# Attention logits in one visit to full-height matmuls per chunk, and two value loads moved in their queue

## The chip, the cores and the metric

The kernel runs on one NeuronCore of a Trainium2 chip. The metric is the device time of one execution in microseconds (us). TensorE is called PE in the profile (PEld are its weight loads), VectorE is DVE, ScalarE is ACT, GpSimd is POOL and SyncE is SP. POOL and SP issue nearly all DMAs here: what POOL issues runs on the queue that the profile calls q0, what SP issues on q1.

## What is computed

One block of a conditioned transformer: modulation rows from a condition `c`, a local dilated attention with 32 heads of 18 channels, and a bilinear gated feed-forward layer. S is 2048, D is 576, F is 4608, everything in bf16.

```python
mod = (silu(c) @ w_mod).reshape(1, 6, 1, -1)      # sa, ca, ga, sb, cb, gb
h = layernorm(x) * (1 + ca) + sa
q, k, v = split_heads(h @ wqkv)                    # H=32, Dh=18
idx = pos[:, None] - arange(8)[None, :] * 2        # 8 keys, 2 apart
logits = einsum('bhsd,bhswd->bhsw', q, k[idx]) * scale
attn = softmax(where(idx >= 0, logits, -1e9))
o = einsum('bhsw,bhswd->bhsd', attn, v[idx])
x = x + ga * (o @ wo)
h = layernorm(x) * (1 + cb) + sb
x = x + gb * (((h @ w_gate) * (h @ w_up)) @ w_down)
```

## The kernel before

**Tiling.** The rows are cut into 8 chunks of 256 (numbered 0 to 7) for the attention, and into five groups of 128-row tiles for the feed-forward layer (`GROUPS`: 256, 512, 512, 384 and 384 rows; group 0 to 4). For each group `gate_up` makes gate and up products for 36 column tiles f of F, then `down` multiplies by `w_down`. The attention of chunks 1 to 7 is cut into small pieces that are put between the column tiles of those two loops: chunks 1 and 2 in group 0, 3 and 4 in group 1, 5 and 6 in group 2, 7 in group 3. Everything is emitted by hand in one order, and each engine executes its own instructions in that order.

**The main loop, and its two kinds of matmuls.** `gate_up` computes with half-height matmuls (`half`, L523): the contraction is split into rows 0 to 63 and rows 64 to 127 of the array, two matmuls run at the same time, one for the gate and one for the up product. A column tile takes 9 such pairs. In the page these are `pg` and `pu`, line L524, form 64\*128. The attention pieces use all 128 rows: the logits (`b_lq`, L443) and the transposes (`b_lt`, L459).

**Attention of one chunk.** `b_p(i, w)` (L429) makes on DVE the product of q and of k shifted by window step w, one tile of 128 x 1280 in bf16 (L433); there are eight, and the pool `prodp` holds six. `b_lq(i, wq)` (L437) sums four of those products over the channels of a head with 20 matmuls against the 0/1 matrix `ind` into the PSUM tile `lg`, one half (wq = 0 or 1) of it at a time. After the second half ACT copies `lg` to `lgs` (L449). `b_lt` transposes `lgs` with four matmuls, then comes the softmax on DVE and ACT (`b_sm0`, `b_exp`, `b_sm1`), then the weighting of the shifted values by `b_mul` (L496) and their sum by `b_add`. The shifted values are loaded by `b_ld(i, j)` (L421, issued at L427 on POOL's queue: 1152 KB, one load for each half j of a chunk) into the two buffers `vsh` of `vshp`.

**Order.** `B_two` and `B_one` (L706, L710) write out the order of the pieces of two chunks, or of one, with a cost beside each (0.83 for a product, 0 for `b_lq`, and so on). `spread` (L735) places a piece at the column tile where the middle of its cost falls, in proportion to the sum of all costs. In column tile k PE runs the first half of tile k, the second half of tile k-1, and then the pieces of slot k; DVE runs the pieces of slot k and then the product `hh` of tile k-1 (L778), which waits for the two casts of ACT (L772, L773).

**Loads.** `load_wgu` (L145) loads a block of four column tiles of `w_gate` and `w_up` on SP's queue; three buffers, and `ahead` (L790) issues block n+2 when block n-1 is done. `load_wd` (L160) loads a block of `w_down` on POOL's queue, again three buffers. `behind(dma, load)` (L181) makes one DMA wait until a given load has landed. `gb_row` (L1144) runs in `down` of group 0, after its first tile: it makes the row `gb` from `wm5`, a tile that holds one of the three `w_down` buffers, and then issues the loads of `w_down` blocks 1 and 2 and the value loads of chunk 2.

Of the kernel before, what the change touches and what calls it, by code (L numbers as in the profile page):

```python
# [7 lines left out]
BF = mybir.dt.bfloat16  # L8
# [10 lines left out]
P = 128  # L19
D = 576  # L20
DP = 640
KT = 5
# [10 lines left out]
CH = 256  # L33
ST = CH // P
# [12 lines left out]
def kernel(  # L47
# [20 lines left out]
    def pool(name, bufs, **kw):  # L68
        return ctx.enter_context(tc.tile_pool(name=name, bufs=bufs, **kw))
# [6 lines left out]
    lnp = pool("lnp", 2)  # L76
# [4 lines left out]
    prodp = pool("prodp", 6)  # L81
# [10 lines left out]
    def ps(shape, dt, name):  # L92
        return psp.tile(shape, dt, name=name, tag="bank")
# [21 lines left out]
    oT = consts.tile([P, KT, CH], BF, name="oT")  # L115
# [13 lines left out]
    def x_rows(i):  # L129
        return x_flat[i * CH:(i + 1) * CH, :].rearrange("(j p) d -> p j d", p=P)  # L130

    def load_x(i):
        if i < NCH:
            x_in[i] = sp.tile([P, ST, D], BF, name="x_t1") if i == 1 else xin.tile([P, ST, D], BF, name="x_t")
            nc.sync.dma_start(x_in[i][:], x_rows(i))
# [5 lines left out]
    wgu_blk, wgu_in, wd_blk = {}, {}, {}  # L141
    NG = len(GROUPS)
    NBLK = FT // FB
# [16 lines left out]
    def load_wd(g):  # L160
        if g >= NG * NBLK - 4:
            return
        r0 = (g % NBLK) * FB * P
        wb = wdp.tile([P, FB, D], BF, name="wd")
        wd_blk[g] = wb
        return nc.gpsimd.dma_start(wb[:], B_w_down[r0:r0 + FB * P, :].rearrange("(k p) n -> p k n", p=P))  # L166
# [14 lines left out]
    def behind(dma, load):  # L181
        tc.add_manual_dep(dma.ins, load.ins.name, SYNC, reason="value rows go first")
# [93 lines left out]
    def layernorm(src, tag):  # L276
        xn, stat, rsq, norm = ln_parts(src, tag)
        for j in range(ST):
            stat(j)

        def norms(js=range(ST)):
            for j in js:
                norm(j)
        return xn, lambda: rsq(slice(0, ST)), norms
# [13 lines left out]
    def transposed(src, dst, cols, vi, between=None, kf=KF):  # L298
        n = P * len(cols)
        pA = ps([P, 3, n], BF, "tr_pA")  # L300
        pB = ps([P, 2, n], BF, "tr_pB")
        for c, j in enumerate(cols):
            if c and between:
                between()
            for m in range(KT):
                d = pA[:, m, :] if m < 3 else pB[:, m - 3, :]
                nc.tensor.transpose(d[:, js(c)], src[:, j, m * P:(m + 1) * P], ident[:])  # L307

        def evict(on_dve=(0, 1, 2)):
            for m in range(KT):  # L310
                s = pA[:, m, :] if m < 3 else pB[:, m - 3, :]
                modulate(dst(m), s, kf if m == KF else m, vi + 1, vi, m in on_dve)
        return evict
# [32 lines left out]
    def a_ln(i):  # L346
        x = x_in.pop(i)
        xn, rsq, norm = layernorm(lambda j: x[:, j, :], "a")
        aa[i] = dict(xn=xn, rsq=rsq, norm=norm)

    def a_norm(i):
        aa[i]["rsq"]()
        aa[i]["norm"]()

    def a_tiles(i):
        hT = hTp.tile([P, KT, CH], BF, name="hT") if i > 1 else vshp.tile([P, KT, CH], BF, name="vsh")
        aa[i].update(hT=hT, qT=qTs[i % 2], kT=kTs[i % 2])
# [8 lines left out]
    def a_t(i, on_dve=(0, 1, 2), between=None):  # L366
        a_tiles(i)
        hT = aa[i]["hT"]
        transposed(aa[i]["xn"], lambda m: hT[:, m, :], (0, 1), 0, between, KT if i in PAIRED else KF)(on_dve)
# [51 lines left out]
    def b_ld(i, j):  # L421
        b = bb.setdefault(i, dict(prod={}, vsh={}))
        base = HALO + i * CH + j * P - DIL * (W - 1)
        vsh = vshp.tile([P, W, DH, H], BF, name="vsh")
        vsrc = bass.AP(vd.tensor, vd.offset + base * D, [[D, P], [DIL * D, W], [1, D]])
        b["vsh"][j] = vsh
        return nc.gpsimd.dma_start(vsh[:].rearrange("p w d h -> p w (d h)"), vsrc)  # L427

    def b_p(i, w):  # L429
        b = bb.setdefault(i, dict(prod={}, vsh={}))  # L430
        off = HALO - DIL * (W - 1 - w)
        prod = prodp.tile([P, KT, CH], BF, name="prod")
        nc.vector.tensor_tensor(prod[:], aa[i]["qT"][:], aa[i]["kT"][:, :, off:off + CH], ALU.mult)  # L433
        b["prod"][w] = prod


    def b_lq(i, wq):  # L437
        b = bb[i]
        if wq == 0:
            b["lg"] = ps([P, 2, CH], F32, "lg")  # L440
        for m in range(KT):
            for wl in range(4):
                nc.tensor.matmul(b["lg"][H * wl:H * (wl + 1), wq, :], lhsT=ind[:, m, :], rhs=b["prod"][4 * wq + wl][:, m, :],  # L443
                                 start=(m == 0), stop=(m == KT - 1), skip_group_check=True)
        for wl in range(4):
            b["prod"].pop(4 * wq + wl)
        if wq == 1:
            lgs = lgp.tile([P, 2, CH], BF, name="lgs")
            nc.scalar.copy(lgs[:], b.pop("lg")[:])  # L449
            b["lgt"] = lgp.tile([P, 2, ST, 4, H], BF, name="lgt")  # L450
            b["lgs"] = lgs

    def b_lt(i):
        b = bb[i]
        lgs = b.pop("lgs")
        pt = ps([P, 2, ST, P], BF, "lt")
        for a in range(2):
            for j in range(ST):
                nc.tensor.transpose(pt[:, a, j, :], lgs[:, a, js(j)], ident[:])  # L459
        nc.scalar.copy(b["lgt"][:].rearrange("p a j w h -> p (a j w h)"), pt[:].rearrange("p a j n -> p (a j n)"))  # L460

    def b_sm0(i):
        b = bb[i]
        lg = b.pop("lgt")
        mx = smp.tile([P, ST, 4, H], BF, name="mx", tag="tree")
        dd = smp.tile([P, 2, ST, 4, H], F32, name="dd")
        nc.vector.tensor_tensor(mx[:], lg[:, 0], lg[:, 1], ALU.max)
        nc.vector.tensor_tensor(mx[:, :, 0:2], mx[:, :, 0:2], mx[:, :, 2:4], ALU.max)
        nc.vector.tensor_tensor(mx[:, :, 0], mx[:, :, 0], mx[:, :, 1], ALU.max)
        for wq in range(2):  # L470
            nc.vector.tensor_tensor(dd[:, wq], lg[:, wq], mx[:, :, 0:1].to_broadcast([P, ST, 4, H]), ALU.subtract)
        b["dd"] = dd
# [221 lines left out]
    def B_pr(i, w0, w1):  # L694
        return [(0.83, lambda w=w: b_p(i, w)) for w in range(w0, w1)]

    def B_lq(i, wq):
        return [(0.0, lambda: b_lq(i, wq))]

    def B_sm(i, beside=None):  # L700
        return [(0.5, lambda: (b_lt(i), beside and beside())),  (1.2, lambda: b_sm0(i)), (0.8, lambda: b_exp(i)), (0.4, nop), (1.8, lambda: b_sm1(i))]

    def B_wait(us):
        return [(us, nop)]

    def B_two(a, b, av_a, av_b, turned=None):  # L706
        return (B_pr(a, 0, 6) + B_lq(a, 0) + B_pr(a, 6, 8) + B_pr(b, 0, 2) + B_lq(a, 1) + B_pr(b, 2, 6) + B_sm(a, lambda: b_lq(b, 0))
                + B_pr(b, 6, 8) + av_a[:4] + B_lq(b, 1) + av_a[4:] + B_sm(b, (lambda: a_t(turned)) if turned else None) + av_b)

    def B_one(a, ld, av_a):  # L710
        return B_pr(a, 0, 4) + ld[:1] + B_pr(a, 4, 6) + B_lq(a, 0) + B_pr(a, 6, 8) + ld[1:] + B_wait(1.5) + B_lq(a, 1) + B_wait(4.0) + B_sm(a) + av_a

    def B_av(i):
        r = []
        for j in range(ST):
            r += [(0.7, lambda j=j, w=w: b_mul(i, j, w)) for w in range(0, W, 2)]
            r += [(0.7, lambda j=j: b_add(i, j, 0)), (0.7, lambda j=j: b_add(i, j, 1)), (1.2, lambda j=j: b_add(i, j, 2))]
            if i in (3, 5):
                r.append((0.0, lambda j=j: b_ld(i + 1, j)))
        return r  # L720
# [402 lines left out]
    def res(i):  # L1123
        return (0.0, lambda: load_res(i))

    def values(i):
        return [(0.0, lambda: [b_ld(i, j) for j in range(ST)])]

    gbg = {0: B_two(1, 2, B_av(1) + [res(2), (0.0, load_wm5), (0.0, lambda: load_wd(0))], []),
           1: values(3) + B_two(3, 4, B_av(3) + [res(3), res(4), (2.4, lambda: a_ln(5)), (1.2, lambda: (a_norm(5), load_x(7)))], B_av(4), 5),  # L1130
           2: values(5) + B_two(5, 6, B_av(5) + [res(5), res(6)], B_av(6)),
           3: B_one(7, [(0.0, lambda j=j: b_ld(7, j)) for j in range(ST)], B_av(7)) + [res(7)],
           4: [(1.0, nop), (1.0, early_wd)]}
    av2 = [p for _, p in B_av(2)]
    oq = out_qkv(1, 3)
# [8 lines left out]
    def gb_row():  # L1144
        mod_row(lambda p, k: wm5[p, k, :] if k < KF else wm5r[p, :], gb_bc, sc_bc2)()
        behind(load_wd(1), wgu_in[4])
        behind(b_ld(2, 0), wgu_in[7])
        b_ld(2, 1)
        load_wd(2)

    dbg = {0: [gb_row] + first + out_qkv(2, 4) + [load_pair_rows],
           1: out_qkv(3, 5) + out_qkv(4, 6),
# [43 lines left out]
```

## Time and profile before

| | us |
|---|---|
| median of 3 runs | 558.31 (557.96 to 561.82) |
| the profiled execution, its own time | 557.38 |
| its span in the profile | 555.7 |
| PE busy in the span | 547.4 (99%) |
| DVE busy | 330.5 (59%) |
| ACT busy | 251.6 (45%) |
| DMA moved | 108.38 MB, 195 GB/s on average |

Windows of the trace give the start of each stage: gate and up products of group 0 from 48.8 us, of group 1 from 131.6, of group 2 from 256.1, of group 3 from 379.5 and of group 4 from 472.5. The granted TensorE clock is full in all 40 slices of the page. A row of the trace's timeline reads: start, duration, engine, line, operation, output and inputs, tile form on the array, shape and count; in square brackets the idle time of that engine just before it and what ended it. The end of a matmul is modelled, so the distance between the starts of neighbouring matmuls is the better measure of what they cost.

### The profile page before, as it was taken

What the parts mean: (1) busy time and instruction counts of PE and PEld (TensorE: products, weight loads), DVE (VectorE), ACT (ScalarE), POOL (GpSimd) and SP (SyncE); (2) the same over time, 40 slices, a digit from 0 to 9 for tenths busy, and PEclk for the clock granted to TensorE, in tenths of its full rate; (3) what the DMA queues carried; (4) which work ended last, traced back from release to release, by engine and by line L of the source; (5) the groups of instructions that cost most, each with busy time, mean ns of one, the idle gap of its engine ahead of it and who ended that gap; (6) DMA issues with size and microseconds to landing.
All of it is one profiled execution on the core that took longest, in us unless ns stands there. A gap on an engine that the chain in (4) does not pass through costs nothing.

```text
span 555.7 us, 14629 instructions
## 1 busy us (share of the span) xinstructions
PE 547.4 (99%) x6195; PEld 323.0 (58%) x6195; DVE 330.5 (59%) x796; ACT 251.6 (45%) x592; POOL 63.2 (11%) x98
## 2 busy tenths in 40 slices
PE   8999999999999999999999999999999999999997
PEld 5877886665444465555544445556656555556564
DVE  7888898976677763546468686445527714322202
ACT  2746665344565663212655553114556511455500
POOL 3103001123001001112000001111200022200010
PEclk9999999999999999999999999999999999999999
DMA  8999999656637734436625945444585665975031
GB/s 277 285 291 316 347 295 354 192 172 205 217 123 246 239 132 141 127 95 220 212 82 159 329 142 155 129 124 133 177 289 183 190 194 179 319 221 191 2 86 32
DMA packets 70155, 108.38 MB, mean 195 GB/s; under 512 B 3690, under 2 KB 57850, under 8 KB 70090
## 3 DMA queue, kind: packets, MB, share of 16 engines
q1 hardware_dynamic: 58832, 61.50, 36.3%
q0 software_dynamic: 11168, 45.81, 26.0%
q8 instruction: 48, 0.79, 0.6%
q14 instruction: 17, 0.14, 0.1%
q10 hardware_dynamic: 90, 0.15, 0.1%
HBM read 103.00 MB, written 4.44 MB: 193 GB/s over the span
## 4 chain that ended last, share of the span: by engine, by line
PE 81%; DMA 5%; issue 3%; DVE 1%; POOL 0%; ACT 0%; SPq 0%; POOLq 0%
PE pg L524 25%; PE acc L814 21%; PE pu L524 20%; DMA wgu<-in_B_w_up_dram 4%; PE pp L524 4%; PE accr L818 3%; PE pw L669 2%; PE pq L385 2%; DMA wd<-in_B_w_down_dram 1%; PE lg L443 1%; PE pv L408 1%; PE tr_pA L307 1%; PE oT_pA L516 0%; PE tr_pB L307 0%; DVE o_t L853 0%
## 5 line engine op out<-in xcount | busy, mean ns | idle before, releaser
L524 PE MATMUL pg<-h2T,wgu 64*128 64x512 bf16 (+2 forms) x1440 | 279.4, 333 | 0.0
L524 PE MATMUL pu<-h2T,wgu 64*128 64x512 bf16 (+2 forms) x1440 | 278.0, 333 | 0.8 <-DMA wgu<-in_B_w_up_dram 0.8
L524 PEld LDWEIGHTS <-wgu 64*128 64x128 bf16 x2880 | 140.3, 94 | 105.8 <-DMA wgu<-in_B_w_up_dram 1.2
L772 ACT CAST u_sb<-pu 128x512 bf16<-128x512 f32 (+2 forms) x180 | 90.2, 501 | 133.3 <-PE pg L524 130.8
L814 PE MATMUL acc<-wd,hh 128*128 128x512 bf16 (+1 forms) x548 | 134.8, 372 | 0.4 <-DMA wd<-in_B_w_down_dram 0.4
L778 DVE TENSOR_TENSOR hh<-g_sb,u_sb 128x512 bf16<-128x512 bf16 (+2 forms) x180 | 66.7, 372 | 108.6 <-ACT g_sb L773 107.2
L818 PE MATMUL accr<-wd,hh 128*128 128x64 bf16 x528 | 93.7, 193 | 0.0
L773 ACT CAST g_sb<-pg 128x512 bf16<-128x512 f32 (+2 forms) x180 | 91.5, 508 | 0.0
L814 PEld LDWEIGHTS <-hh 128*128 128x128 bf16 x588 | 55.2, 98 | 59.6 <-issue 1.7
L524 PE MATMUL pg<-h2T,wgr 64*128 64x512 bf16 (+2 forms) x180 | 60.2, 335 | 0.2 <-DVE h2T L294 0.2
L524 PE MATMUL pu<-h2T,wgr 64*128 64x512 bf16 (+2 forms) x180 | 60.2, 335 | 0.0
L166 POOL DMA_DIRECT2D wd<-in_B_w_down_dram x41 | 30.9, 753 | 245.3 <-PE accr L818 228.0
L818 PEld LDWEIGHTS <-hh 128*128 128x128 bf16 x576 | 51.7, 98 | 2.1 <-issue 0.5
L433 DVE TENSOR_TENSOR prod<-qT,kT 128x1280 bf16<-128x1280 bf16 x56 | 44.8, 818 | 8.1 <-ACT kT L364 4.3
L496 DVE TENSOR_TENSOR vsh<-vsh,attn 128x1152 bf16<-128x1152 bf16 x56 | 40.6, 751 | 0.0
L524 PEld LDWEIGHTS <-wgr 64*128 64x128 bf16 x360 | 17.6, 94 | 16.9 <-issue 4.7
L427 POOL DMA_DIRECT2D vsh<-vd x14 | 12.5, 894 | 110.1 <-DVE o_sb L507 78.2
L671 DVE TENSOR_TENSOR x<-pw,ga_bc 128x512 bf16<-128x512 f32 x14 | 9.6, 689 | 25.7 <-PE pw L669 25.7
L294 DVE TENSOR_SCALAR h2T<-tr_pA,modc 128x256 bf16<-128x256 bf16 (+1 forms) x27 | 8.8, 383 | 26.2 <-PE tr_pA L307 26.2
L267 ACT ACTIVATE ln_rstdb<-ln_mvb,eps 128x2 f32<-128x2 f32 (+1 forms) x9 | 2.7, 295 | 44.0 <-DVE ln_mvb L264 44.0
L296 ACT ACTIVATE h2T<-tr_pB,modc 128x256 bf16<-128x256 bf16 (+1 forms) x16 | 7.7, 535 | 30.2 <-PE tr_pB L307 30.2
L503 DVE TENSOR_TENSOR vsh<-vsh 128x1152 bf16<-128x1152 bf16 x28 | 20.5, 751 | 0.0
(215 smaller groups left out, 540.1 us busy)
## 6 DMA issues: line engine op xcount, KB each, us to landing
wd<-in_B_w_down_dram POOLq DMA_DIRECT2D x41, 576.0 KB, 4.5
wgu<-in_B_w_gate_dram SPq DMA_DIRECT2D x45, 512.0 KB, 4.3
wgu<-in_B_w_up_dram SPq DMA_DIRECT2D x45, 512.0 KB, 5.7
vsh<-vd POOLq DMA_DIRECT2D x14, 1152.0 KB, 9.0
x_r<-in_A_x_dram SPq DMA_DIRECT2D x8, 288.0 KB, 7.0
vsh<-in_B_w_down_dram POOLq DMA_DIRECT2D x4, 576.0 KB, 9.2
out_dram<-x SPq DMA_DIRECT2D x15, 144.0 KB, 4.6
x_t<-in_A_x_dram SPq DMA_DIRECT2D x7, 288.0 KB, 6.5
```

The costliest lines, as they stand in the source:

```text
L166: return nc.gpsimd.dma_start(wb[:], B_w_down[r0:r0 + FB * P, :].rearrange("(k p) n -> p k n", p=P))
L385: nc.tensor.matmul(pq[:, gi, :], lhsT=qk_w(kt, m), rhs=hT[:, kt, cols], start=(kt == 0), stop=(kt == KT - 1))
L427: return nc.gpsimd.dma_start(vsh[:].rearrange("p w d h -> p w (d h)"), vsrc)
L433: nc.vector.tensor_tensor(prod[:], aa[i]["qT"][:], aa[i]["kT"][:, :, off:off + CH], ALU.mult)
L496: nc.vector.tensor_tensor(v, v, at, ALU.mult)
L503: nc.vector.tensor_tensor(vsh[:, d], vsh[:, d], vsh[:, 4 + 2 * s:6 + 2 * s], ALU.add)
L524: return nc.tensor.matmul(dst, lhsT=lhs, rhs=rhs, start=first, stop=last, skip_group_check=True)
L772: nc.scalar.copy(u[:, 0:N], pu[:, 0:N])
L773: nc.scalar.copy(g[:, 0:N], pg[:, 0:N])
L778: nc.vector.tensor_tensor(hh[:, f, 0:N], g[:, 0:N], u[:, 0:N], ALU.mult)
L814: nc.tensor.matmul(a[:], lhsT=hh[:, f, js(j)], rhs=wb[:, f % FB, cs], start=(f == 0), stop=(f == FT - 1))
L818: nc.tensor.matmul(accr[:, j, :], lhsT=hh[:, f, js(j)], rhs=wb[:, f % FB, 512:D], start=(f == 0 and j == 0), stop=(f == FT - 1), skip_grou ...
```

## The change

`B_both` takes the place of `B_two` for chunks 3 to 6, and `B_one` (chunk 7) is changed in the same way: all eight products of a chunk come first, and the two halves of the logits run one behind the other (`b_lqs`). Chunks 1 and 2 keep `B_two`. Since eight products are alive at once and `prodp` holds six, for chunks 3 to 7 product 6 is written to `oT` (the tile that later takes the transposed attention output) and product 7 to a tile `ln_xn` of the pool `lnp` (two buffers, otherwise for normalised rows). Three waits of 1.5 in cost are added to the list of groups 1 and 2, so its sum goes from 47.88 to 52.38 in group 1 and from 44.28 to 48.78 in group 2.

Chunk 7's second value load now waits until block 4 of group 3's gate and up weights has landed. In `gb_row` the load of `w_down` block 2 is issued ahead of chunk 2's second value load, no longer after it.

```diff
     def b_p(i, w):
         b = bb.setdefault(i, dict(prod={}, vsh={}))
         off = HALO - DIL * (W - 1 - w)
-        prod = prodp.tile([P, KT, CH], BF, name="prod")
+        if i > 2 and w == 6:
+            prod = oT
+        elif i > 2 and w == 7:
+            prod = lnp.tile([P, KT, CH], BF, name="ln_xn")
+        else:
+            prod = prodp.tile([P, KT, CH], BF, name="prod")
...
+    def b_lqs(i):
+        b_lq(i, 0)
+        b_lq(i, 1)
+
+    def B_both(a, b, av_a, av_b, turned=None):
+        return (B_pr(a, 0, 8) + B_wait(1.5) + [(0.0, lambda: b_lqs(a))] + B_wait(1.5) + B_pr(b, 0, 8) + B_wait(1.5)
+                + B_sm(a, lambda: b_lqs(b)) + av_a + B_sm(b, (lambda: a_t(turned)) if turned else None) + av_b)
+
     def B_one(a, ld, av_a):
-        return B_pr(a, 0, 4) + ld[:1] + B_pr(a, 4, 6) + B_lq(a, 0) + B_pr(a, 6, 8) + ld[1:] + B_wait(1.5) + B_lq(a, 1) + B_wait(4.0) + B_sm(a) + av_a
+        return (B_pr(a, 0, 4) + ld[:1] + B_pr(a, 4, 8) + ld[1:] + B_wait(1.5) + [(0.0, lambda: b_lqs(a))] + B_wait(4.0) + B_sm(a) + av_a)
...
-           1: values(3) + B_two(3, 4, B_av(3) + [res(3), res(4), ...], B_av(4), 5),
-           2: values(5) + B_two(5, 6, B_av(5) + [res(5), res(6)], B_av(6)),
-           3: B_one(7, [(0.0, lambda j=j: b_ld(7, j)) for j in range(ST)], B_av(7)) + [res(7)],
+           1: values(3) + B_both(3, 4, B_av(3) + [res(3), res(4), ...], B_av(4), 5),
+           2: values(5) + B_both(5, 6, B_av(5) + [res(5), res(6)], B_av(6)),
+           3: B_one(7, [(0.0, lambda: b_ld(7, 0)), (0.0, lambda: behind(b_ld(7, 1), wgu_in[3 * NBLK + 4]))], B_av(7)) + [res(7)],
...
         behind(load_wd(1), wgu_in[4])
         behind(b_ld(2, 0), wgu_in[7])
+        load_wd(2)
         b_ld(2, 1)
-        load_wd(2)
```

More of the change, by code (lines that the diff above doesn't have):

```diff
@@ L1129 @@
     gbg = {0: B_two(1, 2, B_av(1) + [res(2), (0.0, load_wm5), (0.0, lambda: load_wd(0))], []),
-           1: values(3) + B_two(3, 4, B_av(3) + [res(3), res(4), (2.4, lambda: a_ln(5)), (1.2, lambda: (a_norm(5), load_x(7)))], B_av(4), 5),
-           2: values(5) + B_two(5, 6, B_av(5) + [res(5), res(6)], B_av(6)),
-           3: B_one(7, [(0.0, lambda j=j: b_ld(7, j)) for j in range(ST)], B_av(7)) + [res(7)],
+           1: values(3) + B_both(3, 4, B_av(3) + [res(3), res(4), (2.4, lambda: a_ln(5)), (1.2, lambda: (a_norm(5), load_x(7)))], B_av(4), 5),
+           2: values(5) + B_both(5, 6, B_av(5) + [res(5), res(6)], B_av(6)),
+           3: B_one(7, [(0.0, lambda: b_ld(7, 0)), (0.0, lambda: behind(b_ld(7, 1), wgu_in[3 * NBLK + 4]))], B_av(7)) + [res(7)],
            4: [(1.0, nop), (1.0, early_wd)]}
```

## The prediction, made before the changed kernel ran

> **What bounds the kernel.** I read the page first: its busy times, then the chain that ended last.
>
> ```profile
> PE 547.4 (99%) x6195; PEld 323.0 (58%) x6195; DVE 330.5 (59%) x796; ACT 251.6 (45%) x592; POOL 63.2 (11%) x98
> ...
> PE 81%; DMA 5%; issue 3%; DVE 1%; POOL 0%; ACT 0%; SPq 0%; POOLq 0%
> ```
>
> PE carries the span and nothing else comes near. A busy PE is no proof of a full one, so I went through the starts of neighbouring matmuls. In a column tile of groups 1 and 2 pairs start 0.215 us apart; from 132 us on larger steps stand only at visits to full-height matmuls, at the ends of stages and at one DMA wait; `down` of group 0, ahead of that, has another. Whatever the change wins must come from those places. One visit of the logits, in the timeline of PE:
>
> ```profile
> 138.25 0.38 PE L524 MATMUL pg<-h2T,wgu 64*128 64x512 bf16 x1
> 138.56 0.73 PE L443 MATMUL lg<-prod,ind 128*32 128x256 bf16 x20
> 139.22 0.39 PE L524 MATMUL pg<-h2T,wgr 64*128 64x512 bf16 x1
> ...
> 139.45 0.38 PE L524 MATMUL pg<-h2T,wgu 64*128 64x512 bf16 x1
> ```
>
> From 138.25 to 139.45 are 1.20 us, where two steps of 0.215 would be 0.43: a visit costs 0.77. The 20 matmuls are five sets of four that share the array. The whole visit lasts 0.73 and one matmul 0.27 (the line's median), so the sets start (0.73 - 0.27)/4 = 0.11 apart and fill 5 x 0.11 = 0.55. What is left, 0.77 - 0.55 = **0.22 us, is paid for going there and back**. Chunk 7's visit, in a group with narrower pairs (0.162), gives the same: from 405.13 to 406.21 are 1.08, less 2 x 0.162, less 0.55 is 0.21.
>
> The first DMA wait is in group 3, the second in `down` of group 0:
>
> ```profile
> 410.60 0.32 PE L524 MATMUL pg<-h2T,wgu 64*128 64x384 bf16 x1
> 411.77 0.33 PE L524 MATMUL pu<-h2T,wgu 64*128 64x384 bf16 x1 [0.84 <-DMA wgu<-in_B_w_up_dram]
> ```
>
> ```profile
> 97.76 0.19 PE L818 MATMUL accr<-wd,hh 128*128 128x64 bf16 x1
> 98.33 0.38 PE L814 MATMUL acc<-wd,hh 128*128 128x512 bf16 x1 [0.38 <-DMA wd<-in_B_w_down_dram]
> ```
>
> In the first, 411.77 would have been 410.76: 1.01 us lost. In the second the next start is otherwise 0.03 later (97.52 to 97.55): 0.54 lost.
>
> **The visits.** Before, chunks 3 and 4 make five visits (logits; logits; transposes of 3 with logits of 4; logits; transposes of 4 with chunk 5's), chunks 5 and 6 five, chunk 7 three. After: three, three and two. Five journeys fewer at 0.22: **1.10 us**. All 200 logit matmuls of these chunks stay. Bounds: nothing if the cost goes with the matmuls and not with the journey, 5 x 0.77 = 3.9 if the second half were free, which its five sets exclude. A visit that joins two things already is in the trace: last pair 149.50, four transposes and 20 logits, next pairs 150.80 and 151.02. It costs 1.52 - 0.43 = 1.09; the transposes fill 0.24 (x4 in 0.40 us, one takes 0.22, so 0.06 apart), the logits 0.55, and 0.30 is left, not the 0.41 of two journeys (transposes alone, 414.38 to 415.13: 0.75 - 0.325 - 0.24 = 0.19). So the cost goes with the journey, with 0.1 for the change of form inside; logits behind logits change no form.
>
> **The products.** The DVE count stays at 56 products of 0.82 us; a target of `oT` or `ln_xn` has the same shape. Their former users are done: `oT` was last read in `down` of the group before, and of `lnp`'s two buffers each is taken after its transposes. So 0, and a DVE that is 59% busy hides it; what it costs uncovered is the wait of the visit itself. A merged visit needs product 7, so it waits if DVE is late, and behind it on PE stands the whole main loop. By the costs, product 7 and the visit are 0.415 + 1.5 = 1.9 apart: 1.3 column tiles in group 1, 1.4 in group 2, 2.4 in group 3; never in one slot. In group 1 product 7 is in slot 4 and the visit in slot 5, at 131.6 + 5.5 x 1.94 = 142.3 us. DVE's rows:
>
> ```profile
> 139.77 0.42 DVE L778 TENSOR_TENSOR hh<-g_sb,u_sb 128x512 bf16<-128x512 bf16 x1 [0.78 <-ACT g_sb L773]
> ...
> 145.91 0.83 DVE L433 TENSOR_TENSOR prod<-qT,kT 128x1280 bf16<-128x1280 bf16 x1 [1.06 <-PE lg L443]
> ```
>
> Slot 3 now has two products where it had one, and the second (0.78) fills just the 0.78 that DVE was idle ahead of the first row. So this `hh` still ends at 140.2 and product 7, next behind it, at 141.0, 1.3 before its use. The second row is a wait that goes away: product 6 of a chunk asked for a buffer of the first visit. The next chunk's first product asks for it instead, a slot after the merged visit, when this (1.3 us long) has ended. One new wait is certain: `b_sm0` of chunks 3 and 5 falls into the slot of its own transposes (12 and 13; before, one slot later), so DVE waits for ACT's casts and copy there, some 2 us, with `hh` of that tile behind it. ACT's casts have three buffers and PE eight banks, and the slots around it hold one short piece or none: 0. All later pieces move by one slot or two, and their DMAs with them: chunk 4's value loads from slots 17 and 21 to 19 and 22, chunk 6's by one each; the row loads of chunks 3 to 7 go past one weight block on SP. A value load lands 9.0 us after its issue in the median, 4.6 slots, and chunk 4's halves are read from slots 28 and 32: 0 again; uncovered, DVE would wait there with `hh` behind it.
>
> **Chunk 7's value load.** The queues' rows, SP's and POOL's:
>
> ```profile
> 399.31 1.66 SPq L151 DMA_DIRECT2D wgu<-in_B_w_up_dram  x1
> ```
>
> ```profile
> 396.39 1.80 POOL L427 DMA_DIRECT2D vsh<-vd  x2 [3.03 <-DMA vd<-v_sb]
> ```
>
> Two value loads of 1152 KB go out at 396.4 and 397.3 and land after 9.1 and 12.3 us; block 4, issued at 399.3, lands at 411.7. From 403 to 411 the DMA moves 349 to 360 GB/s, all its engines busy. With 1.18 MB taken out, block 4 is there 1.18/0.355 = 3.3 us sooner, at 408.4, against a need at 410.76: **1.01 us** won whole, the lower bound 0. The load held back goes from 408.4 beside block 5, needed near 416.4. Before, the backlog is through by 413.5; the same bytes in other order end no later. The load's first reader is DVE at 432.4. POOL waits at `behind`, and nothing stands behind it on POOL before `down`.
>
> **The swap in group 0.** POOL's rows:
>
> ```profile
> 85.25 0.88 POOL L427 DMA_DIRECT2D vsh<-vd  x1 [5.49 <-DVE hh L778]
> 90.30 0.76 POOL L166 DMA_DIRECT2D wd<-in_B_w_down_dram  x1 [4.17 <-PE pb L332]
> ```
>
> Block 2 of `w_down` waits for PE's `gb` row until 90.3 either way. Now the value load stands behind it: it goes out at 91.1, not 85.25, and lands not before 98 to 101 (its reader: 105.3). Block 2 had 8.0 us to land behind that load; alone in its queue, with half of the 355 GB/s, 0.59 MB take 3.3 us: there by 95, need 97.8, and the 0.54 are won. But block 3 (issued at 93.9, landed at 101.0, needed at 101.87) is now behind the value load in time as well, and its need comes 0.54 sooner, at 101.33. DMA is saturated until 99 and drained at 102 (32 GB/s from there), so block 3 lands between 101.0 and 102.0 and gives back 0 to 0.7. I take **0.3 net**, nearer to the upper end since q1, alone from 87.6 (chunk 2's first value load landed, 8.7 after 78.87) to 91, runs dry first and leaves the rest to q0.
>
> **Sum.** 1.10 + 1.01 + 0.3 = 2.4 us: a span of 553.3, the profiled execution at 557.38 - 2.4 = 555.0. The median of the runs lies 0.93 above the profiled one: 558.31 - 2.4 = **555.9**.
>
> **The rivals.**
> *Block 3 late (slower than before).* q0 and q1 share evenly to the end, q1 never runs dry. Then block 2, the value load and block 3, 2.36 MB, go from 91 at 178 GB/s until 104.3, 3.0 after the need: 558.31 - 1.10 - 1.01 - 0.54 + 3.0 = 558.7. It decides when block 3 lands later than 101.33 + 2.65 = 104.0. Against it: before, the same queue brought the same bytes by 101.0 with q1 busy beside it, and q1 has all bandwidth from 87.6 to 91. The Trainium skill, in "DMA: Bandwidth & Descriptors", section "Issuing engines are not separate DMA queues", says that DMAs of all issuing engines run on the same 16 engines and interleave; by it alone the swap only hands lateness on, which is this rival. The trace bears out the sharing: two queues at once, 355 GB/s together. Chance 0.15.
> *Product 7 late (slower too).* Slack is 1.3 us in group 1. If DVE lags one more column tile, 1.94, each of the four visits of groups 1 and 2 waits 0.6: 558.31 - 2.4 + 2.6 = 558.5; two tiles, 2.6 each: 566.2. It decides from a lag of 1.3 + 2.4/4 = 1.9 on. Against it: DVE's waits for `g_sb`, 0.5 to 0.8 us in most tiles from 135 to 151, show it ahead of ACT, not behind. 0.08.
> *Nothing saved per journey.* The merged visit costs 2 x 0.77: only the DMA terms, 558.31 - 1.3 = 557.0. 0.10.
> *The forecast*, with the DMA terms between their bounds (gain 1.8 to 2.65): 0.62. The other 0.05 is for what I don't see.
>
> **Numbers.** Low: the profiled 557.38 less 2.65 is 554.7, rounded to 554.5; high: 559.0 takes in the late block (558.7) and a DVE one tile late (558.5). About 1%, 5.6 us, is what a measurement of this kernel can tell from no change. Faster by that would need more than the journeys of all 13 visits (2.9) and both DMA waits (1.55) together: 0.03. Slower by it: half of the late-product case and part of the unseen: 0.07. The rest, 0.90, within.
>
> **What would show it.** Right: `lg` in rows of x40 with some 1.10 us of fill and the same 0.22 around it; no DMA wait of PE at 98 and 411; group 3 starting 4 x 0.22 + 0.3 = 1.2 us ahead of 379.5. Wrong: idle PE ahead of `lg` ended by DVE `prod`; a wait on `wd` near 101; a step over 0.12 between sets in the second half of a visit.

## The result, and the profile after

The changed kernel takes 556.01 us in the median of 22 runs (555.14 to 557.58), the kernel before 558.00 (22 runs, 556.96 to 561.82): a ratio of 0.9958, with a 95% interval of 0.9948 to 0.9968, or 2.3 us less by 0.6 either way. The profiled execution of the changed kernel took 556.14 us, with a span of 554.4.

The busy times and the chain of the page after:

```profile
PE 544.1 (98%) x6160; PEld 323.9 (58%) x6195; DVE 330.5 (60%) x796; ACT 251.8 (45%) x592; POOL 63.7 (11%) x98
...
PE 84%; DMA 9%; DVE 6%; ACT 1%; issue 1%; SPq 0%
```

PE still carries the span. Its row holds 6160 of the 6195 matmuls (the weight loads are all there), so its busy time can't be set against the one before. New in the chain is DVE, at 6% where it had 1%; where that lies is shown with the swap below. The spans, 555.7 and 554.4, say little too, because they hold something that the change does not touch: the stretch up to the first gate weights took 48.80 us in the trace of before and 49.62 in that of after, and between 48.6 and 50.5 over the fourteen profiles of this study, whose instructions up to there are the same. The comparison therefore goes by stages, each measured from the first weight load of one stage to that of the next (us):

| stage | before | after | difference |
|---|---|---|---|
| group 0, `gate_up` and `down` | 82.74 | 82.96 | +0.22 |
| group 1, `gate_up` | 81.29 | 80.85 | -0.44 |
| group 2, `gate_up` | 80.50 | 80.06 | -0.44 |
| group 3, `gate_up` | 62.53 | 61.14 | -1.39 |
| group 4, `gate_up` | 52.76 | 52.76 | 0 |
| `down` of groups 1 to 4, each | | | at most 0.01 |

Together -2.05, which agrees with the -2.3 of the runs. One merged visit of the logits, in the timeline of PE:

```profile
143.18 0.38 PE L529 MATMUL pg<-h2T,wgu 64*128 64x512 bf16 x1
143.48 0.83 PE L448 MATMUL lg<-prod,ind 128*32 128x256 bf16 x22
...
144.05 0.27 PE L448 MATMUL lg<-ln_xn,ind 128*32 128x256 bf16 x1
...
144.16 0.27 PE L448 MATMUL lg<-ln_xn,ind 128*32 128x256 bf16 x1
...
144.49 0.27 PE L448 MATMUL lg<-ln_xn,ind 128*32 128x256 bf16 x1
144.69 0.39 PE L529 MATMUL pg<-h2T,wgr 64*128 64x512 bf16 x1
```

The matmuls appear under three names, since products 6 and 7 now lie in `oT` and `ln_xn`; each row of `ln_xn` is the end of one set of the second half, and these lie 0.11 apart to the last. From pair to pair are 144.69 - 143.18 = 1.51 us. Less one pair (0.215) and ten sets of 0.109, 0.205 are left: one journey, where there were two. No idle time stands ahead of `lg`.

The place of the first DMA wait, in group 3, on PE, and POOL's rows of chunk 7's value loads:

```profile
410.37 0.32 PE L529 MATMUL pg<-h2T,wgr 64*128 64x384 bf16 x1
...
410.53 0.32 PE L529 MATMUL pg<-h2T,wgu 64*128 64x384 bf16 x1
...
410.70 0.32 PE L529 MATMUL pg<-h2T,wgu 64*128 64x384 bf16 x1
```

```profile
396.36 0.90 POOL L427 DMA_DIRECT2D vsh<-vd  x1 [2.85 <-DVE hh L791]
406.69 0.90 POOL L427 DMA_DIRECT2D vsh<-vd  x1 [9.43 <-DVE hh L791]
```

The pairs run on at 0.16; the second value load goes out ten microseconds after the first instead of one. The gate half of block 4, issued at 399.05, landed after 5.7 us, where it had taken 11.3.

The place of the second wait, in `down` of group 0, first on PE and then on POOL:

```profile
98.59 0.19 PE L831 MATMUL accr<-wd,hh 128*128 128x64 bf16 x1
98.61 0.38 PE L827 MATMUL acc<-wd,hh 128*128 128x512 bf16 x1
...
101.64 0.19 PE L831 MATMUL accr<-wd,hh 128*128 128x64 bf16 x1
101.87 0.38 PE L827 MATMUL acc<-wd,hh 128*128 128x512 bf16 x1
```

```profile
91.11 0.76 POOL L166 DMA_DIRECT2D wd<-in_B_w_down_dram  x1 [10.55 <-PE pb L332]
91.87 0.89 POOL L427 DMA_DIRECT2D vsh<-vd  x1
94.70 0.76 POOL L166 DMA_DIRECT2D wd<-in_B_w_down_dram  x1 [1.95 <-PE accr L831]
```

A step from `accr` to `acc` is 0.025 without a wait. Block 2 of `w_down` is now in time (0.02 from 98.59 to 98.61, where 0.57 stood), and block 3, issued at 94.70 behind the value load, is 0.23 - 0.025 = 0.205 late. So, counted from the start of group 0, PE is 0.54 - 0.205 = 0.33 ahead of the kernel before at this point; yet the stage ends 0.22 later. This is the part of the prediction that did not come.

### The profile page after: what moved, and what is told of

It reads as the page before. It is cut to its first block, busy times and chain, and to the rows that moved or that the text cites. A ratio compares the mean times of both kernels' runs of the same rounds, so it can differ in the third digit from the quotient of the medians.

```text
span 554.4 us, 14594 instructions
## 1 busy us (share of the span) xinstructions
PE 544.1 (98%) x6160; PEld 323.9 (58%) x6195; DVE 330.5 (60%) x796; ACT 251.8 (45%) x592; POOL 63.7 (11%) x98
## 4 chain that ended last, share of the span: by engine, by line
PE 84%; DMA 9%; DVE 6%; ACT 1%; issue 1%; SPq 0%
PE pg L529 28%; PE pu L529 22%; PE acc L827 19%; PE pp L529 4%; PE accr L831 3%; DMA wgr<-in_B_w_gate_dram 3%; PE pw L674 2%; DMA wo<-in_A_wo_dram 2%; PE lg L448 2%; DMA wgu<-in_B_w_gate_dram 1%; DMA x_t<-in_A_x_dram 1%; DVE vsh L501 1%; PE pq L385 1%; DVE ln_xn L272 1%; DMA wmA<-in_w_mod_dram 1%
## 5 line engine op out<-in xcount | busy, mean ns | idle before, releaser
L827 PE MATMUL acc<-wd,hh 128*128 128x512 bf16 (+1 forms) x522 | 131.0, 372 | 0.2
L438 DVE TENSOR_TENSOR prod<-qT,kT 128x1280 bf16<-128x1280 bf16 x46 | 37.1, 828 | 4.3 <-ACT kT L364 4.3
```

The costliest lines, as they stand in the source:

```text
L827: nc.tensor.matmul(a[:], lhsT=hh[:, f, js(j)], rhs=wb[:, f % FB, cs], start=(f == 0), stop=(f == FT - 1))
```

## The experiments

In all of them except the one that computes the logits twice, the same things are computed as in the kernel before. Medians stand beside runs of the kernel before on the same chip; the ratios are to those.

**The journeys: the two halves apart again.** Eight products, `oT` and `ln_xn` as in the change, but a column tile or more between the halves.

```diff
-        return (B_pr(a, 0, 8) + B_wait(1.5) + [(0.0, lambda: b_lqs(a))] + B_wait(1.5) + B_pr(b, 0, 8) + B_wait(1.5)
-                + B_sm(a, lambda: b_lqs(b)) + ...
+        sm = B_sm(a, lambda: b_lq(b, 0))
+        return (B_pr(a, 0, 8) + B_wait(1.5) + B_lq(a, 0) + B_wait(1.5) + B_lq(a, 1) + B_pr(b, 0, 8) + B_wait(1.5)
+                + sm[:2] + B_lq(b, 1) + sm[2:] + ...
```

(`B_one` in the same way.)

> The changed kernel with its eight products first and both DMA edits, but the two halves of the logits of chunks 3 to 7 one column tile apart again: five visits more. Stages are measured from the first gate product of a group to the first product of the down loop behind it (group 1: 81.29 us before, 80.85 after the change; group 2: 80.50 and 80.06; group 3: 62.53 and 61.14). Theory (0.22 us for each journey to full-height matmuls and back): 81.29, 80.50 and 61.36, together 1.10 more than the changed kernel, ratio to before about 0.998. Rival (the cost goes with the matmuls, and the gain came from the order of the products): 80.85, 80.06, 61.14.

Groups 1, 2 and 3 take 81.29, 80.50 and 61.36 us: 0.44, 0.44 and 0.22 more than in the changed kernel, to the hundredth the lengths of before in groups 1 and 2. Timed: 556.89 (11 runs), ratio 0.9980 (0.9971 to 0.9989). Each of the five added visits costs 0.22, and the eight products held at once cost nothing, since they are still held here.

**The journeys: twice the matmuls in a visit.** The other side of the same claim: if the cost goes with the journey, more matmuls in the same visit cost only their own time. The logits of chunks 3 to 7 are computed twice, the second time over the first.

```diff
-        for m in range(KT):
-            for wl in range(4):
...
+        for _ in range(2 if i > 2 else 1):
+            for m in range(KT):
+                for wl in range(4):
...
```

> The changed kernel in which chunks 3 to 7 compute each half of the logits twice, the second time over the first, so that a visit has 80 matmuls in place of 40. Theory (0.22 us for each journey, 0.109 for each set of four matmuls, however many): each of the five visits is 10 x 0.109 = 1.09 longer; stages from the first gate product to the first down product: group 1 80.85 + 2.18 = 83.03, group 2 82.24, group 3 62.23. Rival (sets late in a long visit start further apart, since PE's instructions are there ahead of time only so far): clearly over 83.2 in group 1, with sets over 0.12 apart in the trace.

The first visit in its timeline:

```profile
144.23 1.38 PE L449 MATMUL lg<-prod,ind 128*32 128x256 bf16 x42
...
146.33 0.27 PE L449 MATMUL lg<-ln_xn,ind 128*32 128x256 bf16 x1
146.53 0.39 PE L530 MATMUL pg<-h2T,wgr 64*128 64x512 bf16 x1
```

Eighty matmuls keep the pace of 0.109 for a set. Groups 1, 2 and 3 take 83.03, 82.25 and 62.23: 2.18, 2.19 and 1.09 more than in the changed kernel, which is 1.09, or ten sets of 0.109, for each visit. The journey does not grow with what is done there. (There was one run, 562.35 us.)

**The hold, taken out.**

```diff
-           3: B_one(7, [(0.0, lambda: b_ld(7, 0)), (0.0, lambda: behind(b_ld(7, 1), wgu_in[3 * NBLK + 4]))], B_av(7)) + [res(7)],
+           3: B_one(7, [(0.0, lambda: b_ld(7, 0)), (0.0, lambda: b_ld(7, 1))], B_av(7)) + [res(7)],
```

> The changed kernel with chunk 7's second value load no longer held behind weight block 4. Theory (the two value loads at once make the block late): PE waits about 1.0 us again near 410, group 3 takes 62.1 to 62.4 us in place of 61.14, groups 1 and 2 stay. Rival (the block is in time anyhow once the logits are one visit): 61.14.

```profile
410.76 0.32 PE L529 MATMUL pg<-h2T,wgu 64*128 64x384 bf16 x1
411.04 0.33 PE L529 MATMUL pu<-h2T,wgu 64*128 64x384 bf16 x1
```

In the profiled execution the `pu` of a pair, which should start with its `pg`, came 0.28 late, and group 3 takes 61.42, less than the 62.1 to 62.4 that I had expected; the same place had cost 1.17 in the profile of before. Timed, 557.59 (12 runs, 556.65 to 561.22), ratio 1.0002 (0.9987 to 1.0017): by the ratios 2.5 us behind the changed kernel (0.0044 of 558). Three of these runs (559.82, 559.88 and 561.22) have a mean granted clock of 0.996 or 0.997 where the other nine have 0.999 or more, so their length need not come from a wait; but the median of the nine is 557.51, so the loss does not hang on them. The profiled execution was the shortest of the twelve, and in it POOL's queue was late too, in group 0:

```profile
101.20 0.19 PE L831 MATMUL accr<-wd,hh 128*128 128x64 bf16 x1
102.65 0.38 PE L827 MATMUL acc<-wd,hh 128*128 128x512 bf16 x1 [1.25 <-DMA wd<-in_B_w_down_dram]
```

Here block 3 of `w_down` is 1.43 late, on the same instructions that waited 0.205 for it in the changed kernel, and the stage takes 83.63, 0.67 more. Waits of this kind are no constants.

**The same kernel in a second profile**, to see whether the wait in group 3 or something else carries the timed loss.

> The changed kernel without the hold once more, in a second profiled execution (first one: group 3 at 61.42 us, 0.28 longer than with the hold, but a median 1.6 us above the changed kernel's). Theory (how far the two value loads and block 4 of group 3's weights get into each other's way differs from one execution to the next): groups 1, 2 and 4 keep 80.85, 80.06 and 52.76, only group 3 takes another length, between 61.1 and 63.7; median 556.5 to 558. Rival (the stall is 0.28 always, and something else that the hold moves, in group 4 or ahead of group 3, carries the rest of the timed loss): group 3 61.4 again and another stage longer by 1 us or more. Second rival (the first median was of a bad set of runs): median 556.0 to 556.4, group 3 61.4.

Group 3 takes 61.25, only 0.11 above the changed kernel's, and all other stages are the changed kernel's (82.97, 80.84, 80.06, 52.76). Median 557.05 (12 runs, 555.81 to 559.26), ratio 0.9980 (0.9964 to 0.9996), 1.2 us behind the changed kernel by the ratios. So the same code lost 0.28 and 0.11 in its two profiles. Neither profile shows the whole timed loss in group 3: in the first, group 0 lost 0.67 as well; the second, 557.08 us, is 0.92 above the profile of the control further down (the changed kernel once more), and 0.80 of that lies in the stretch up to the first gate weights (50.40 us against 49.60), which the hold does not touch. The single runs spread over 3.45 us, from 555.81, which is no more than the changed kernel's middle. This fits a wait that differs from one execution to the next. The profiles caught only small ones; that a large one stands behind the longer of these runs is inferred, not seen.

**The hold alone**, in the kernel before.

```diff
-           3: B_one(7, [(0.0, lambda j=j: b_ld(7, j)) for j in range(ST)], B_av(7)) + [res(7)],
+           3: B_one(7, [(0.0, lambda: b_ld(7, 0)), (0.0, lambda: behind(b_ld(7, 1), wgu_in[3 * NBLK + 4]))], B_av(7)) + [res(7)],
```

> The kernel before, with nothing changed but that chunk 7's second value load waits for weight block 4. Theory (the hold removes the whole wait at block 4, 1.17 us in the profile before, and a wait that differs from execution to execution): group 3 takes 62.53 - 1.17 = 61.36, and the timed median is 1 to 2.4 us under before, ratio 0.9955 to 0.998, with less spread. Rival (the wait was mostly a matter of that one profile, 0.3 us as in the profile of the changed kernel without the hold): ratio 0.9995 or above.

Group 3 takes 61.36, 1.17 less than before. Timed 556.88 (12 runs), ratio 0.9982 (0.9971 to 0.9994): 1.0 us faster. Its profiled execution was its slowest, 558.52, and the trace shows why. Group 4, in the timeline of PE:

```profile
489.23 0.32 PE L524 MATMUL pg<-h2T,wgu 64*128 64x384 bf16 x1
490.62 0.33 PE L524 MATMUL pu<-h2T,wgu 64*128 64x384 bf16 x1 [1.07 <-DMA wgu<-in_B_w_up_dram]
```

1.39 us are lost (the next expectation has 1.23, one pair of 0.16 less). I took it for another collision of the same sort, with the four early loads of `w_down` (`early_wd`), which the change does not touch: they go out from 473.3 on and land 8 to 11 us later, and the weights that PE waits for, issued at 479.50, land after 11.1 us. In the changed kernel the same loads go out together and the weights land after 9.5 us, in time. In no other profile with these loads in their old place does this wait appear.

**The early loads held back as well**, so that the collision just seen cannot happen.

```diff
-                nc.gpsimd.dma_start(wb[:, k], ...)
+                r = nc.gpsimd.dma_start(wb[:, k], ...)
+                if n == NBLK - 4 and k == 0:
+                    behind(r, wgu_in[4 * NBLK + 4])
```

> The changed kernel, and the four loads of w_down that are issued at the start of group 4 (2304 KB at once) also wait, until block 4 of that group's gate and up weights has landed. Theory (these four loads are the same collision as chunk 7's value loads, and PE waits for a weight block in some executions only: 1.23 us in the profile of the kernel before with the hold alone): group 4 takes 52.76 in the profile as without it, the lowest time stays, the slower executions go, median 0.2 to 0.5 us lower than the control. Rival (the spread comes from elsewhere): no difference of medians over 0.2 us.

> The changed kernel once more, beside the two runs that follow on the same chip. Theory: stages from the first gate product to the first down product as in its first profile (group 1 80.85, group 2 80.06, group 3 61.14, group 4 52.76), median 555.4 to 556.4 us. If DMA waits of PE come and go from execution to execution, group 0's down loop (43.63) or group 4 may differ by up to 1.5 us.

(The second is the changed kernel itself, run beside it.) The control reproduced its stages within 0.01 and took 555.86 (8 runs, 555.25 to 556.62). The held version took 556.40 (12 runs), ratio 0.9974 (0.9963 to 0.9985) against 0.9965: not 0.2 to 0.5 lower, as I had expected, but 0.5 higher (the two intervals overlap). In its group 4:

```profile
505.32 0.32 PE L531 MATMUL pg<-h2T,wgu 64*128 64x384 bf16 x1
505.82 0.33 PE L531 MATMUL pu<-h2T,wgu 64*128 64x384 bf16 x1 [0.17 <-DMA wgu<-in_B_w_up_dram]
```

The `pu` is 0.50 late, and group 4 takes 53.26 where the control takes 52.76: now that the four loads go out at 490.4, a later block of weights is late. Behind chunk 7's held load no block was late; here one was.

**The swap, taken out.**

```diff
-        load_wd(2)
         b_ld(2, 1)
+        load_wd(2)
```

> The changed kernel with block 2 of w_down again behind chunk 2's second value load. The stretch from the first gate product of group 0 to the first of group 1 took 82.71 us before and 82.94 after the change, in one profile each. Theory (DVE sets the pace of the down loop of group 0 from 96 to 118 us, so what PE no longer waits for at block 2 it waits for later): PE loses 0.5 us again at block 2, none at block 3, and the stretch stays within 0.25 us of 82.8. Rival (the swap is worth its 0.3 us and the profile hid it): 0.3 us or more longer than the changed kernel, 83.2.

```profile
98.88 0.19 PE L831 MATMUL accr<-wd,hh 128*128 128x64 bf16 x1
99.77 0.38 PE L827 MATMUL acc<-wd,hh 128*128 128x512 bf16 x1 [0.70 <-DMA wd<-in_B_w_down_dram]
```

PE lost 0.89 - 0.025 = 0.865 at block 2, more than the 0.545 of before. Yet the stage takes 83.06, against 82.96 and 82.97 in the changed kernel and its control: of 0.865 us, 0.1 shows, and the stage is 0.26 over 82.8, just outside what I had expected. Timed 555.87 (5 runs), ratio 0.9964 (0.9952 to 0.9976), within 0.0001 of the control's. The swap is worth 0.1 or less here. The cover has an end, though: the kernel before lost 0.545 at the same block and took 82.74, so the 0.32 that this wait is longer shows in full.

The control adds the other half: with the swap in, its block 3 was in time (101.62 to 101.65, a step of 0.03), 0.2 better than in the first profile of the same kernel, and the stage was no shorter, 82.97.

```profile
101.62 0.19 PE L831 MATMUL accr<-wd,hh 128*128 128x64 bf16 x1
101.65 0.38 PE L827 MATMUL acc<-wd,hh 128*128 128x512 bf16 x1
```

Who sets the pace then? The chain of waits of the changed kernel (start, duration, engine, tile, line) runs over DVE from 88.9 to 118, with a step on ACT now and then; in the chain of before there is no DVE in this stretch, but PE and its wait for block 2. With that wait PE is about level with DVE; without it, DVE is the later one.

```profile
88.88 0.29 DVE hh L791
...
112.59 0.96 DVE h2T L294 x3
...
116.04 1.41 DVE ln_xn L272 x4
117.45 0.61 DVE x L676
118.10 1.24 PE pw L674 x5
```

DVE's rows at both ends of the stretch, after and then before:

```profile
89.09 0.42 DVE L487 TENSOR_TENSOR ss<-dd 128x256 f32<-128x256 f32 x1
...
112.50 1.04 DVE L294 TENSOR_SCALAR h2T<-tr_pA,modc 128x256 bf16<-128x256 bf16 x3
```

```profile
88.28 0.42 DVE L482 TENSOR_TENSOR ss<-dd 128x256 f32<-128x256 f32 x1
...
111.69 1.04 DVE L294 TENSOR_SCALAR h2T<-tr_pA,modc 128x256 bf16<-128x256 bf16 x3
```

Both distances are 23.41 us, although PE went through the same stretch with other waits. DVE works through its list here with no idle time above 0.04 but 0.60 for ACT's `ln_rstda`, which itself waits for DVE. PE meets DVE again at the transposes of `ln_xn` at 109, where what PE had won is waited off. After, and then before:

```profile
108.80 0.28 PE L307 MATMUL tr_pB<-ident,ln_xn 128*128 128x128 bf16 x2
109.15 0.34 PE L307 MATMUL tr_pA<-ident,ln_xn 128*128 128x128 bf16 x3
```

```profile
108.31 0.27 PE L307 MATMUL tr_pB<-ident,ln_xn 128*128 128x128 bf16 x2
108.42 0.33 PE L307 MATMUL tr_pA<-ident,ln_xn 128*128 128x128 bf16 x3
```

The step is 0.35 after and 0.11 before. Counted from the start of `down`, PE comes to these transposes 0.31 ahead of the kernel before in the changed kernel, 0.52 in its control and 0.16 in the split; it leaves them 0.07, 0.07 and 0.06 ahead. A PE that comes later than in the kernel before (by 0.12 with the doubled logits, 0.33 without the swap, 0.89 in the run that lost 1.43) leaves them exactly as late. So DVE covers a wait of some 0.45 us in this stage, and not more. Then the stage loses something. DVE's normalisation behind that, and POOL's row beside it, after:

```profile
L272 DVE TENSOR_SCALAR ln_xn<-x_t,ln_mva,ln_rstda x4: 282/352/661, 116.0 to 117.2; 128x576 bf16<-128x576 bf16 x2, 128x64 bf16<-128x64 bf16 x2
```

```profile
115.85 0.75 POOL L166 DMA_DIRECT2D wd<-in_B_w_down_dram  x1 [1.39 <-PE accr L831]
116.04 1.41 DVE L272 TENSOR_SCALAR ln_xn<-x_t,ln_mva,ln_rstda 128x576 bf16<-128x576 bf16 x4 [0.60 <-ACT ln_rstda L268]
```

and before:

```profile
115.11 0.85 POOL L166 DMA_DIRECT2D wd<-in_B_w_down_dram  x1 [1.39 <-PE accr L818]
115.23 1.19 DVE L272 TENSOR_SCALAR ln_xn<-x_t,ln_mva,ln_rstda 128x576 bf16<-128x576 bf16 x4 [0.60 <-ACT ln_rstda L268]
```

The three numbers of the first row are the shortest, the median and the longest duration in ns: the first of the four took 0.66 us, where the longest of before took 0.43 at this place. In after POOL began to issue its DMA 0.20 ahead of it; in before 0.12 ahead, and there it was POOL's row that was longer, 0.85 instead of 0.75. Of the fourteen profiles, five have POOL 0.19 or 0.20 ahead here (the changed kernel, its control, the split, the held early loads, the second look without the hold), and all five show the long DVE row (0.66 or 0.67); in the other nine POOL is at most 0.12 ahead, or behind, and the row takes 0.43. POOL's issue is released by PE. What is left of PE's lead behind the transposes at 109 is 0.07, just what POOL's lead has grown by, and with it DVE comes out 0.24 later and the stage ends 0.22 later. The same meeting stands at 94 us in all fourteen profiles, the kernel before included:

```profile
L272 DVE TENSOR_SCALAR ln_xn<-x_t,ln_mva,ln_rstda x4: 283/364/630, 93.6 to 94.7; 128x576 bf16<-128x576 bf16 x2, 128x64 bf16<-128x64 bf16 x2
```

There POOL is 0.22 to 0.25 ahead of the second row of 576 columns, which takes 0.62 to 0.65. In all nineteen cases the DVE row ends 0.11 after POOL's; with POOL 0.35 ahead or more, or 0.12 or less, a row of 576 columns takes 0.42 or 0.43. The Trainium skill, in "SBUF — State Buffer", section "SBUF: two separate sides", says that DVE in its two-port modes and GpSimd take a port pair by an exclusive lock, and whichever starts first makes the other wait. The trace agrees in that DVE ends 0.11 after POOL whatever the lead between 0.19 and 0.25; it does not agree at a lead of 0.12, where POOL started first and DVE did not wait. That it is this port was not tested.

**DVE relieved, with the swap and without it.** The test of the pace. For chunk 3 the three scalings behind the transposes (1.04 us on DVE) go to ACT.

```diff
-        return (... + [o[1], lambda: a_t(n), o[2], o[3]] + ...
+        return (... + [o[1], lambda: a_t(n, () if n == 3 else (0, 1, 2)), o[2], o[3]] + ...
```

> The changed kernel, and of chunk 3's modulated transposes the three evictions that DVE made (0.35 us each, 1.04 together, at 98 us) go to ACT, which idles 4.2 us there. Theory (DVE sets the pace of the down loop of group 0): PE's waits for ln_xn near 109 and for the bank of pw near 118 go, 0.3 to 0.5 us, and the stretch from the first gate product of group 0 to the first of group 1 falls to about 82.4 us. Rival (DMA or PE itself sets the pace): 82.9 as it is, or longer, if ACT hands chunk 3's hT over later.

> The run with chunk 3's evictions on ACT (stretch from the first gate product of group 0 to the first of group 1: 82.22 us), and in addition w_down block 2 again behind chunk 2's second value load. Theory (the swap's gain was real on PE, 0.5 to 0.85 us at block 2 less 0.2 at block 3, and was given back only because DVE set the pace): with DVE relieved the wait at block 2 stays in the total, the stretch is 82.5 to 82.9. Rival (the swap is worth nothing in any case): 82.2.

With the swap the stage takes 82.22, 0.74 less than in the changed kernel (0.24 of it is the long DVE row, which takes 0.43 here, since POOL begins 0.03 behind it); without it 82.77, and there block 2 is 0.575 late. So with DVE out of the way the swap is worth 0.55, which is that lateness; with DVE in the way it was worth 0.1 or less. That settles the pace. Timed, the two take 555.75 (12 runs) and 556.01 (8 runs), ratios 0.9970 (0.9957 to 0.9982) and 0.9967 (0.9951 to 0.9983): 0.5 us is not to be told apart by these runs. And the stage is not the whole: in all 44 runs of the four versions with chunk 3's scalings on ACT (these two and two below) the device time is 1.98 to 2.09 us longer than the span, in all other runs of the changed kernel and its variants 1.65 to 1.78. So 0.3 us of what the stage wins is lost outside the span, for a reason that stays open.

**Further on the same way.** The transposes of chunk 3 one piece later as well, and that together with the held early loads.

```diff
-        return (... + [o[1], lambda: a_t(n), o[2], o[3]] + ...
+        return (... + ([o[1], o[2], lambda: a_t(n, ()), o[3]] if n == 3 else [o[1], lambda: a_t(n), o[2], o[3]]) + ...
```

> The run with chunk 3's evictions on ACT, and in addition chunk 3's ten transposes come after chunk 1's second output projection, no longer ahead of it. Theory (the transposes wait 0.6 us for DVE's ln_xn, and the projection fills that time): the stretch from the first gate product of group 0 to the first of group 1 falls from 82.22 to about 81.7 us. Rival (DVE or the next step on ACT is late in its place, since ACT hands chunk 3's hT over some 1.4 us later): 82.2 or more.

> The changed kernel with chunk 3's evictions on ACT, chunk 3's transposes behind chunk 1's second output projection, and the four early w_down loads held. Theory (the first two take 1.0 us out of the stretch from the first gate product of group 0 to the first of group 1, 81.96 in place of 82.96): a median 1.0 us or more under the control. Rival (what the profile shows there is lost to the start of the kernel, which differs by over 1 us between profiles): medians within 0.4 us.

The first takes 81.96 in the stage, 1.0 less than the changed kernel, where I had expected 81.7; the second 82.12 there, and 53.50 in group 4, where the held loads cost 0.74 (504.64 to 505.38). Timed: 555.66 (12 runs, 554.54 to 558.57), ratio 0.9967 (0.9952 to 0.9981), and 556.05 (12 runs), ratio 0.9966 (0.9953 to 0.9979). The second is not 1.0 under its control but 0.2 over it: its stages win 0.85 and lose 0.74, and the 0.3 outside the span comes on top. No version is shown to beat the changed kernel: the control has 0.9965.

## Why the prediction was right, and where it was not

Predicted 555.9, measured 556.01: the total is right, from 1.10 + 1.17 - 0.22 = 2.05 in the stages instead of 1.10 + 1.01 + 0.3 = 2.4. That it agrees to 0.1 us is luck: the 2.4 were taken off 558.31, the median of three runs, and over 22 runs the kernel before takes 558.00. And the sign that group 3 would start 1.2 us ahead of 379.5 did not show: it starts at 379.66, which is 0.66 ahead once both are counted from the first gate weights. The 1% that I took for the least that a measurement could tell was too wide: the interval of these runs is 0.1% to either side.

- **The visits, 1.10.** Right to the hundredth: two journeys fewer in each of groups 1 and 2, one in group 3, at 0.22. Both rivals on this ground fall: *nothing saved per journey* by the split and by the doubled visits, *product 7 late* because no PE wait stands ahead of `lg` in any of the five visits (in the first, product 7 ended at 141.97, 1.5 before the visit), and groups 1 and 2 are shorter by the journeys exactly. The wait of `b_sm0` for its casts, which I called free, was free.
- **The hold, 1.01.** The mechanism was right, the size a little small: 1.17 in both profiles with the hold that can be set against before. I took the next start at 411.77 against 410.76, one pair too far: the `pu` that waited belongs to the pair whose `pg` started at 410.60. But "won whole" treated one execution's wait as the kernel's own: without the hold the same place cost 0.28 and 0.11 in two other profiles. The runs' verdict is 1.0 (the hold alone) and 1.2 and 2.5 (its removal).
- **The swap, 0.3 net: the step that failed.** Its account of the DMAs held. Block 2's 0.54 were won, block 3 gave back 0.205, and PE was 0.33 ahead at 102 (block 3's need stood at 101.38 in before, not at 101.87 as I had it, so 0.2 was the lower end of what it could give back). What failed is the step from there to the end, "a DVE that is 59% busy": I used a share of the whole span, and looked at DVE's rows only in groups 1 to 3. In `down` of group 0 DVE has hardly any idle time, so PE's wait of 0.545 was covered but for 0.07, and removing it was worth no more than that; behind it came the 0.24 of DVE beside POOL. So the term came out at -0.22 in place of +0.3. The relief of DVE, with and without the swap, showed the cover.
- *Block 3 late*, the rival on the slower side. The mechanism exists: in ten profiles with the swap block 3 was late by 0.2, 0.4, 0.4, 0.65 and 1.43 and five times not at all. The rule that I cited from the Trainium skill ("DMA: Bandwidth & Descriptors", section "Issuing engines are not separate DMA queues"), by which the swap only hands lateness on, is half borne out: without the swap block 2 was late in all four profiles, by 0.55 to 0.87. The 3.0 of the rival did not occur, and the cover by DVE would have taken part of it: the 1.43 lengthened the stage by 0.67 over the changed kernel's.

## What to carry to other kernels

Count the journeys between two forms of matmul and not the matmuls: each journey removed here gave its 0.22 us, at whatever load. Before a wait is priced, look in its own stage for the engine that comes second, because a wait of 0.5 us was worth less than 0.1 where another engine was 0.5 us behind. And a DMA wait seen in one profile is one draw: take its size from several executions, and when a load is moved away from a collision, look for the next block that it will meet.

## What the runs showed of the hardware

- The same instructions up to the first gate weights took 48.6 to 50.5 us in fourteen profiles, nearly as much spread as the whole effect of this change. Stages had to be compared in place of spans.
- A DVE operation of 0.43 us (`tensor_scalar`, 128 x 576 in bf16) took 0.62 to 0.67 when POOL had begun to issue a DMA 0.19 to 0.25 us ahead of it, and ended 0.11 after POOL's row each time (19 of 19). It took 0.42 or 0.43 when POOL's lead was 0.12 or less, or 0.35 or more.
- Eighty matmuls of a full-height visit (160 instructions with their weight loads) ran at 0.109 us for each set of four from first to last.
- The wait for the same DMA, with the same instructions around it, was 0, 0.2, 0.4, 0.65 or 1.4 us in different executions.
